# Two rows of wo per partition loaded early, in sixteen loads of eight partitions

## Chip, cores, metric

The kernel runs on one core of one Trainium2 chip. The metric is the device time of one execution in microseconds. A profile is of one further execution; its span, from the first to the last instruction, is some 2 us shorter than the device time.

## The reference

One decode step: attention over a long cache, plus a small dense block, plus the residual.

```python
q = (xn @ wq)                                   # 2 x 32 heads x 128
scores = einsum("bhqd,bhkd->bhqk", q, k_cache) * (Dh ** -0.5)
o = einsum("bhqk,bhkd->bhqd", softmax(scores), v_cache)
return x + o.reshape(B, 1, H * Dh) @ wo + relu(xn @ w1) @ w2
```

Everything is bfloat16. The caches are 2 x 32 x 8192 x 128 each: 268 MB of the 280.5 MB that the kernel reads. wo is 4096 x 512, 4 MB.

## The kernel before

The work goes in 32 pairs of (batch, head). Each pair has a K tile and a V tile of 4 MB: 128 partitions with 32 KB each. In the trace a tile is 128 packets of 32 KB (a packet is one of its DMA records) and sixteen increments of its semaphore, so eight packets for each of the 16 DMA engines. K and V have two buffers each. PE (TensorE, the matrix engine) transposes the K tile, multiplies it with q, and multiplies the V tile of the pair before with its weights. SyncE (SP) issues all large loads in one queue and waits only for buffers:

```python
        load_k(0)
        load_k(1)
        load_v(0)
        for t in range(NP - 2):
            sp.wait_ge(pT[NG - 1], t + 1)     # K tile t transposed
            load_k(t + R)
            sp.wait_ge(sW, t + 1)             # V tile t - 1 used up
            load_v(t + 1)
        ...                                   # the last V tile in two halves
        for c in range(NC):                   # wo last, in five chunks
            sl = slice(cuts[c], cuts[c + 1])
            sp.dma_start(wo_sb[:, sl, :], wo_v[:, sl, :]).then_inc(dW[c], 16)
```

wo lies in 32 rows of 512 elements (1 KB) per partition. The chunks have 14, 7, 6, 3 and 2 rows, and PE multiplies each with the attention's result as it lands, four matmuls a row:

```python
        for c in range(NC):
            pe.wait_ge(dW[c], 16)
            for j in range(cuts[c], cuts[c + 1]):
                for k in range(KT):
                    t = pe.matmul(fin[:, k, :], lhsT=wo_sb[:, j, k * P:(k + 1) * P],
                                  rhs=OX[:, j, :], start=False, stop=...)
```

## Time and profile before

| what | value | how to read it |
|---|---|---|
| time | 660.92 us (660.84 to 661.13, 6 runs) | median |
| DMA, data queue | 280.50 MB, 99.2% of 16 engines' span | busy all the time: bytes over rate set the end |
| K and V tiles | one lands every 9.71 us | 8 packets of 1.21 us, plus the semaphore write (a packet of 4 B, 9 ns) |
| K tile 4 | lands at 100.80 us | the first tile behind the place of the change |
| last wo chunk | lands at 654.85 us, last of 16 engines | first of them at 653.04 |
| end of PE's matmuls | 655.29 us | 0.44 us behind the landing |

The lines of the page and of the chain that carry this are in the prediction. What matters most is not on the page: the sixteen increments of a load's semaphore. Every load of 128 partitions has sixteen at its landing in the trace. I read each as the end of one DMA engine's share, and their spread as how far the engines have drifted apart. Before, from 130 us on, nine engines are up to 0.4 us apart, and seven are 1.7 to 1.9 us behind the first.

### The profile page before, as it was taken

The page shows a single profiled execution, that of the slowest core. Times are in us where ns is not written, and L with a number is a line of the kernel's source. Part 1 is how long each engine was busy: PE and PEld are TensorE (multiplying, and loading weights), DVE is VectorE, ACT ScalarE, POOL GpSimd, SP SyncE. Part 2 cuts the span into 40 slices and gives each one's busy share as a digit, 9 for nine tenths or more (in the row PEclk, how much of TensorE's full clock was granted, in tenths as well). Part 3 has the DMA queues.
Part 4 walks back from the last instruction along what each step waited for, and adds up shares of the span by engine and source line. Part 5 has one row for each costly group of instructions (what it writes and reads, how often), then busy time and mean ns, then how long its engine had stood idle before and what let it go on. Part 6 is the DMA issues. An engine that isn't in the chain of part 4 may idle for free.

```text
span 658.6 us, 26859 instructions
## 1 busy us (share of the span) xinstructions
PE 559.9 (85%) x12737; PEld 535.1 (81%) x12737; DVE 253.2 (38%) x436; ACT 255.8 (39%) x403; POOL 9.0 (1%) x46
## 2 busy tenths in 40 slices
PE   2998799987989878879887887997878997887896
PEld 0488798987879878879887887987878987887895
DVE  1144344442434433334443343443434443333441
ACT  1043444443433434334353434344333444333340
POOL 1000000000000000000000000000000000000000
PEclk9799999998998988999898899898989998898988
DMA  8999999999999999999999999999999999999996
GB/s 365 430 444 418 439 430 429 432 428 442 422 442 424 436 428 432 432 428 444 420 442 428 432 430 430 434 430 442 424 436 428 432 432 428 440 424 442 426 424 281
DMA packets 10542, 280.66 MB, mean 426 GB/s; under 512 B 1186, under 2 KB 1188, under 8 KB 1700
## 3 DMA queue, kind: packets, MB, share of 16 engines
q1 hardware_dynamic: 10528, 280.50, 99.2%
q8 instruction: 9, 0.15, 0.1%
q14 instruction: 1, 0.01, 0.0%
q10 hardware_dynamic: 4, 0.00, 0.0%
HBM read 280.50 MB, written 0.00 MB: 426 GB/s over the span
## 4 chain that ended last, share of the span: by engine, by line
DMA 58%; PE 37%; ACT 2%; issue 1%; SPq 1%; ACTq 0%; DVE 0%
DMA ks<-in_A_k_cache_dram 54%; PE tp L285 21%; PE Sc L292 11%; PE ot L305 4%; DMA w_sb<-in_A_wo_dram 4%; ACT kT L412 2%; ACT L412 1%; SPq L187 0%; PE Sc L340 0%; SPq L182 0%; PE Sc L343 0%; SPq L170 0%; SPq L169 0%; SPq L163 0%; PE ot L397 0%
## 5 line engine op out<-in xcount | busy, mean ns | idle before, releaser
L285 PE MATMUL tp<-identb,ks 128*128 128x128 bf16 x4096 | 323.5, 229 | 68.4 <-DMA ks<-in_A_k_cache_dram 68.4
L412 DVE COPY kT<-tp 128x1024 bf16<-128x1024 bf16 x320 | 219.7, 691 | 324.3 <-PE tp L285 324.2
L285 PEld LDWEIGHTS tp<-identb,ks 128*128 128x128 bf16 x4096 | 254.8, 102 | 72.3 <-DMA ks<-in_A_k_cache_dram 72.2
L412 ACT COPY kT<-tp 128x1024 bf16<-128x1024 bf16 x192 | 194.3, 1012 | 233.4 <-PE tp L285 233.3
L292 PE MATMUL Sc<-q,kT 128*128 128x64 bf16 x4096 | 216.8, 196 | 7.6 <-ACT kT L412 5.7
L292 PEld LDWEIGHTS Sc<-q,kT 128*128 128x128 bf16 x4096 | 178.4, 100 | 11.3 <-ACT kT L412 9.0
L305 PE MATMUL ot<-prm,vs 128*128 128x64 bf16 x4224 | 156.1, 192 | 4.2 <-issue 4.2
L305 PEld LDWEIGHTS ot<-prm,vs 128*128 128x128 bf16 x4224 | 139.0, 97 | 7.0 <-issue 4.4
L525 ACT COPY nm<-Sc 128x2 f32<-128x2 f32 x32 | 5.1, 160 | 118.5 <-PE Sc L343 118.5
L529 ACT ACTIVATE prm<-Sc,nm 64x128 bf16<-64x128 f32 x64 | 25.7, 401 | 4.3
L466 DVE TENSOR_REDUCE mcol<-Sc 64x1 bf16<-64x128 f32 x64 | 18.6, 290 | 18.7 <-PE Sc L292 18.3
L412 ACT ACT_TABLE_LOAD x16 | 20.5, 1283 | 2.2
L240 PE MATMUL ot<-vs,xz 128*16 128x512 bf16 x32 | 9.5, 470 | 8.6 <-DMA vs<-in_A_wq_dram 8.6
L517 ACT COPY OTf<-ot 128x2 f32 x32 | 5.1, 160 | 26.9 <-PE ot L305 26.9
L471 DVE TENSOR_REDUCE mx<-Sc 1x2 bf16<-1x128 bf16 x32 | 8.9, 278 | 16.9 <-PE Sc L340 16.9
L240 PEld LDWEIGHTS ot<-vs,xz 128*16 128x16 bf16 x32 | 3.3, 105 | 14.4 <-issue 12.2
L225 POOL COPY q<-qb 128x2 bf16<-128x2 bf16 x32 | 5.8, 184 | 588.9 <-PE Sc L292 566.1
L529 ACT ACTIVATION_READ_ACCUMULATOR prm<-Sc,nm x64 | 11.8, 185 | 0.0
L442 DVE TENSOR_SCALAR qs<-ot 16x512 bf16<-16x512 f32 x1 | 0.7, 679 | 18.0 <-PE ot L240 18.0
L340 PE MATMUL Sc<-identb,mcol 128*1 128x128 bf16 x32 | 7.0, 217 | 0.0
L270 PE MATMUL Sc<-w_sb,hT 128*2 128x512 bf16 x14 | 5.8, 604 | 0.1
L343 PE MATMUL Sc<-mx,onesb 1*128 1x2 bf16 x32 | 5.5, 172 | 0.0
(56 smaller groups left out, 37.5 us busy)
## 6 DMA issues: line engine op xcount, KB each, us to landing
ks<-in_A_k_cache_dram SPq DMA_DIRECT2D x32, 4096.0 KB, 26.7
vs<-in_A_v_cache_dram SPq DMA_DIRECT2D x31, 4096.0 KB, 31.3
vs<-in_A_wq_dram SPq DMA_DIRECT2D x1, 4096.0 KB, 12.1
vs<-in_A_v_cache_dram SPq DMA_DIRECT2D x2, 2048.0 KB, 19.3
w_sb<-in_B_w_dram SPq DMA_DIRECT2D x2, 1792.0 KB, 17.9
w_sb<-in_A_wo_dram SPq DMA_DIRECT2D x1, 1792.0 KB, 25.4
w_sb<-in_A_wo_dram SPq DMA_DIRECT2D x1, 896.0 KB, 27.1
w_sb<-in_A_wo_dram SPq DMA_DIRECT2D x1, 768.0 KB, 28.5
```

Source lines behind the costliest of these rows:

```text
L225: g.tensor_copy(q2[t % R][:], qb[:, 2 * t:2 * t + 2]).then_inc(sQ1, 1)
L240: i = pe.matmul(qp, lhsT=xz[:, kt, Z - g * Bsz:Z - g * Bsz + QG * Bsz], rhs=vs[1][:, (kt * QG + g) * 512:(kt * QG + g + 1) * 512], start=( ...
L270: i = pe.matmul(y, lhsT=hT[:, j, :], rhs=w2_sb[:, j, :], start=(j == 0), stop=(j == FT - 1),)
L285: t = pe.transpose(tp[e % 4][:, i, :], ks[r][:, kk * Dh:(kk + 1) * Dh], identb[:])
L292: t = pe.matmul(Sc[r][:, 2 * kk:2 * kk + 2 * REP], lhsT=kT[e % 4][:, i, :], rhs=rep(q2[r][:]), start=True, stop=True,)
L305: t = pe.matmul(ot[r][:, 0:2 * REP], lhsT=vs[r][:, kk * Dh:(kk + 1) * Dh], rhs=rep(prm[r][:, kk, :]), start=(kk == 0), stop=(kk == KB - 1),)
L340: pe.transpose(tr_of(r), mcol[r][:], identb[:]).then_inc(sT, 1)
L343: pe.matmul(bc_of(r), lhsT=onesb[:], rhs=mx[r][:], start=True, stop=True).then_inc(sB, 1)
L412: fn(kT[e % 4][:], tp[e % 4][:]).then_inc(kR[e], 1)
L466: m = v.tensor_reduce(out=mcol[i][half, :], in_=S_of(i)[half, :, u], axis=AX.X, op=ALU.max)
L471: v.tensor_reduce(out=mx[i][:], in_=tr_of(i).rearrange("o (u m) -> o u m", u=2), axis=AX.X, op=ALU.max, negate=True,).then_inc(sX, 1)
L529: x = a.activation(out=prm[i][half, :, u], in_=S_of(i)[half, :, u], func=ACTF.Exp, bias=nm[i][half, u:u + 1], scale=1.0, accum_out=RS[half ...
```

## The change

The intent is to use that drift. Two of the 32 rows of every partition (256 KB) are taken out of the last chunks and loaded in the middle of the stream by eight of the sixteen engines alone, in 16 loads of eight partitions. The trace names no engine. I number the engines by e3 (below), where a load of n partitions ran on n engines for every n from 2 to 16 and each set lay inside the next: engine n - 1 is the one that the load of n partitions adds. That this order holds is my assumption. The low engines are 0 to 7, which carry a load of eight. If they have time to spare, the other eight have 16 KB less to carry at the end. The diff (`...` marks what is left out, here and below):

```diff
...
-    cuts = (0, 14, 21, 27, 30, WJ)
+    cuts = (0, 2, 15, 22, 28, 31, WJ)
+    LOW = 0
...
+    def load_wo(sp, c):
+        step = 8 if c == LOW else P
+        for p in range(0, P, step):
+            sl = slice(p, p + step), slice(cuts[c], cuts[c + 1])
+            sp.dma_start(wo_sb[sl], wo_v[sl]).then_inc(dW[c], 16)
...
             load_v(t + 1)
+            if t == 1:
+                load_wo(sp, LOW)
...
-        for c in range(NC):
-            sl = slice(cuts[c], cuts[c + 1])
-            sp.dma_start(wo_sb[:, sl, :], wo_v[:, sl, :]).then_inc(dW[c], 16)
+        for c in range(1, NC):
+            load_wo(sp, c)
...
-            pe.wait_ge(dW[c], 16)
+            pe.wait_ge(dW[c], 16 * (P // 8) if c == LOW else 16)
```

More of the change, by code (lines that the diff above doesn't have):

```diff
@@ L129 @@
     dH = [sem(f"dH{i}") for i in range(2)]
-    dW = [sem(f"dWo{i}") for i in range(5)]
+    dW = [sem(f"dWo{i}") for i in range(6)]
     sG, sI, sQ, sQ1 = sem("sG"), sem("sI"), sem("sQ"), sem("sQ1")
```

## The prediction

0.30 and 0.32 us less at the end and 16 x 93 ns = 1.49 us more on eight engines take the last landing from 654.85 to about 654.3, and the time from 660.91 to 660.3; with 0.1 us for the rivals it is 660.4.

> **What bounds the kernel now.** I read the page first (parts 2 to 4), then the chain of waits, the DMA queue's own waits, the stretches of the last ten microseconds, and last the sixteen increments of each load's semaphore in the trace.
>
> The page, parts 2 to 4:
>
> ```profile
> DMA  8999999999999999999999999999999999999996
> ...
> q1 hardware_dynamic: 10528, 280.50, 99.2%
> q8 instruction: 9, 0.15, 0.1%
> ...
> DMA 58%; PE 37%; ACT 2%; issue 1%; SPq 1%; ACTq 0%; DVE 0%
> ```
>
> The sixteen DMA engines are busy from the first slice to the last but one. Both directions of the argument start here: 280.50 MB is fixed by the problem, the change adds and removes no byte, so only two things can move: idle time of DMA engines, and what follows the last landing. The last slice (16.5 us) is only 6 tenths busy. The end of the chain, in order of time:
>
> ```profile
> 625.73 29.12 DMA w_sb<-in_A_wo_dram
> 654.85 0.05 issue
> 654.90 0.39 PE ot L397 x8
> 655.29 0.02 issue
> 655.31 0.18 DVE yT L502
> ```
>
> The last of the five wo loads lands at 654.85; eight matmuls (two rows of four) and a fixed output tail follow. Now the DMA share in short stretches there (columns: stretch, length, five engines' busy time with counts, clock, DMA share, GB/s):
>
> ```profile
> 651.00:652.00 1.00, 1.00 (x46) 1.00 (x44) 0.00 (x0) 0.00 (x0) 0.00 (x0) 1.00 1.01 401
> 652.00:653.00 1.00, 0.49 (x18) 0.40 (x14) 0.00 (x0) 0.00 (x0) 0.00 (x0) 1.00 0.83 326
> 653.00:653.40 0.40, 0.15 (x3) 0.07 (x4) 0.00 (x0) 0.00 (x0) 0.00 (x0) 0.68 0.53 215
> 653.40:654.00 0.60, 0.60 (x24) 0.60 (x24) 0.00 (x0) 0.00 (x0) 0.00 (x0) 0.50 0.49 191
> ```
>
> From 653.0 on half of the engines have nothing left, 1.8 us before the other half end. The sixteen increments of the last wo semaphore say the same, in us after its first:
>
> ```
> 0.00 0.02 0.13 0.15 0.16 0.18 0.35 0.40 | 1.63 1.65 1.67 1.70 1.74 1.78 1.80 1.81
> ```
>
> Eight engines end by 653.44, eight at 654.67 to 654.85. For the first weights the spread was 0.38 us in all. The late group grows one by one: the spread jumps to 1.72 us with one late engine in the K tile that lands at 32.73, and there are seven late engines from 130 us to 649 us. What comes in between are packets of the instruction queue. The DMA view of 29 to 110 us, then of 110 to 650 us:
>
> ```profile
> q1 hardware_dynamic: 1205, 34.83, 100.1%
> q8 instruction: 7, 0.11, 0.6%
> ...
> q1 hardware_dynamic: 8342, 232.78, 100.2%
> ```
>
> Seven instruction packets of 16 KB (1.02 to 1.10 us each; the first, at 29.57, also stretched the next data packet from 1.21 to 1.68 us) made seven engines late by about 1.5 us each, and since the queue never runs dry they stay late. The eighth packet, at 650.36, made the eighth. K and V tiles land every 9.71 us throughout, each at the pace of its latest engine.
>
> [...]
>
> **The change part by part.**
>
> *Removed from the end:* one wo row (1 KB) per partition from the first late chunk (14 to 13 rows) and one from the last (2 to 1). Every engine carries 8 partitions. A packet in the trace takes 535 ns at 14336 B, 272 at 7168, 234 at 6144, 121 at 3072, 84 at 2048 (medians), some 38 ns per KB; the 1 KB packets of x took 44. First chunk: 8 x 38 = 0.30 us less. Last chunk: 8 x (84 - 44) = 0.32 us less. All engines that got no early rows end about 0.6 us sooner (16 KB of 4096 KB/16 = 256 KB less).
>
> *Added at 72 us:* on each of 8 engines 16 packets of 2 KB at 84 ns and 16 semaphore writes at 9 ns: 16 x 93 = 1.49 us. They wait in the queue behind V tile 2, which lands at 91.09, and ahead of K tile 4. That the sum is so near the 1.5 us of one instruction packet is why I think that the change was fitted to this skew.
>
> *Sum, if the eight low engines are the early eight:* they end at 653.04..653.44 + 1.49 - 0.6 = 653.9..654.3; the high ones at 654.67..654.85 - 0.6 = 654.1..654.25. Both groups meet, and the last landing goes from 654.85 to about 654.3. Mean work per engine is the same; 0.55 us of the 1.5 us skew's idle time is won.
>
> *After the landing:* four matmuls instead of eight. In the last chunks 24 weight loads took 0.72 us, so four are 0.12 us. Against that, PE has less slack: it was through 84 matmuls at 653.09 and would now have 88 to do before the chunk of 6 rows, landing near 653.0. 24 + 12 + 4 matmuls at 30 to 33 ns from 653.25 on give 654.5, the last 4 after the landing at 654.3 as well. So PE's last matmul moves by 0.6 to 0.7 us, and the output tail stays.
>
> *SP:* the issues that are there take 0.33 to 0.44 us each (the output store of 8 partitions 0.37) with 0.05 between. Sixteen take 16 x 0.42 = 6.7 us, from 71.96 to 78.7. K tile 4 was issued at 83.61, after PE's transposes, so SP is back 4.9 us early.
>
> *Between 91 us and 643 us:* the low engines' half of K tile 4 comes 1.49 us later, level with the late half. The tile landed at 100.80 by its late engines, so it lands within 0.1 us of that. Nothing else in 500 us moves: the late engines set every landing before and after.
>
> The sum is -0.6 us of 660.91, or 660.3; I add 0.1 for the cases below.
>
> **The rivals.**
>
> *The low engines are not the early ones.* Then one late engine gets 1.49 us more and 0.6 us less: 654.85 + 0.9, so 661.8. One low engine among the late is enough. For the good case: the eight instruction packets went to eight different engines, which a blind draw from sixteen would do about one time in eight (16·15·...·9 / 16^8 = 0.12), so they seem to walk a fixed set of eight[...]; and the author's sizes fit it. Against: nothing in the trace names an engine.
>
> *One more instruction packet.*[...] On a late engine it costs 1.5 - 0.6 = +0.9 us; and the packet of 650.36 may fall on an engine without slack. Each is a small chance.
>
> *SP becomes the bound.* If the small loads took 1.1 us each,[...] K tile 4 would be issued after 90 us, V tile 2 would be the last in the queue, and all sixteen engines would idle until it comes. The DMA queue's own waits speak against it: SP waits 429.8 us for PE's transposes in 30 waits. It would cost 1 to 3 us.
>
> *The end is PE's.* If PE falls behind the late chunks, the gain shrinks to 0.3 us.
>
> **Range and chances.** I give 0.72 to the meeting of the two groups (660.0 to 660.7), 0.2 to a late engine made later, by either of the first two rivals (661.6 to 661.9), the rest to no effect or to SP. The three runs of before lie within 0.3 us. Two per cent is 13 us; no mechanism here is above 3 us, so the same within 2% has 0.98.
>
> **What would show it right or wrong.** Right: at the last wo semaphore the sixteen increments lie within 0.6 us instead of 1.81; the share of DMA stays above 0.8 until some 0.4 us before the last landing; that landing at about 654.3; K tile 4 still issued near 83.6; nine instruction packets. From the K tile of 100.8 on, spread below 0.6 us. Wrong: a spread of 3 us at the end with early engines still 1.5 us ahead (low engines were late ones), a tenth instruction packet, SP's issue of K tile 4 after 86 us, or a gap between the last landing and the last matmul over 0.6 us.

## The result, and the profile after

The changed kernel took 663.80 us (662.87 to 664.15, 6 runs) beside 660.92 us: 2.9 us slower, which is 0.4%. Ratios in this document are the mean time of one kernel's fast runs over that of the other's in the same rounds, so not quite the ratio of the medians quoted; here it is 1.0040, with a 95% interval of 1.0027 to 1.0053. "The same within 2%" was right. The predicted 660.4 us and the range up to 661.9 us were wrong.

Where the time goes is plain from the landings. The tiles up to K tile 3 land as before (K tile 3 at 81.58 us, before at 81.38). V tile 2, which was issued ahead of the early rows and carries none of them, lands at 92.37 us instead of 91.09, already 1.3 us late. K tile 4 lands at 104.23 us instead of 100.80, 3.4 us late. From there to the last V half nothing more is lost or won: a tile every 9.71 us again, 3.4 us late. The last wo chunk lands at 657.62 instead of 654.85, 2.8 us late, so the 0.6 us that were to be won at the end did come. The whole loss arises in a few microseconds around 90 us.

There the rate drops. Short stretches of the kernel before, then of the changed kernel (columns: stretch, length, busy time with counts of PE, its weight loads, VectorE, ScalarE and GpSimd, PE's granted clock, DMA share, GB/s):

```profile
88.00:90.00 2.00, 2.00 (x47) 1.86 (x43) 0.37 (x1) 1.10 (x4) 0.00 (x0) 1.00 0.88 377
90.00:92.00 2.00, 1.79 (x43) 1.76 (x43) 1.07 (x3) 1.04 (x2) 0.00 (x0) 1.00 1.18 508
92.00:94.00 2.00, 2.00 (x51) 2.00 (x48) 1.30 (x3) 1.18 (x2) 0.00 (x0) 1.00 0.91 393
```

```profile
88.00:90.00 2.00, 1.79 (x36) 1.62 (x34) 1.20 (x2) 1.17 (x2) 0.00 (x0) 1.00 1.02 316
90.00:92.00 2.00, 2.00 (x51) 2.00 (x49) 0.78 (x2) 1.30 (x2) 0.00 (x0) 1.00 1.06 275
92.00:94.00 2.00, 2.00 (x50) 2.00 (x48) 1.38 (x2) 0.93 (x2) 0.00 (x0) 1.00 0.81 279
```

Single stretches waver, since a packet of 32 KB is counted at one instant (in slices of 0.2 us the rate jumps between 0, 164 and other multiples of 164 GB/s, one such packet); but the three together moved 2.56 MB before and 1.74 MB after (2 us times the sum of the last column), a third less, while the engines counted as busy all along. So they were not waiting for work: their packets took longer. In the trace, the 32 KB packets that started from 88.9 to 96 us took 1.213 to 1.224 us before; after, 42 of 70 took over 1.3 us, and the time above 1.213 us adds up to 21.0 us of engine time. The 2 KB packets took 84 to 255 ns, 113 at the median, where I had reckoned with 84. Large packets of engines that were carrying no small ones were stretched too, as V tile 2 shows.

The second thing to see is who carries the small packets. Six engines begin with them between 88.8 and 89.1 us, when the early engines are through with V tile 2; two begin at 91.05 us. Two of the eight low engines were late ones. The increments of K tile 4, in us after the first (landing of the last in brackets):

```
before (100.80)  0.00 0.11 0.11 0.20 0.20 0.20 0.23 0.24 0.35 0.36 1.69 1.72 1.73 1.76 1.79 1.81
after  (104.23)  0.00 0.08 0.15 0.17 1.25 1.44 1.50 1.60 1.61 1.62 1.69 1.75 1.81 1.86 3.64 3.65
```

Two engines stand 1.8 us behind all others, and they stay last to the end (3.50 and 3.52 us at the last wo chunk, the next at 2.19), and each tile lands with them.

Third, SP. Its timeline in the kernel before (one line), then in the changed kernel:

```profile
83.61 0.33 SPq L158 DMA_DIRECT2D ks<-in_A_k_cache_dram  x1
```

```profile
70.81 0.33 SPq L162 DMA_DIRECT2D vs<-in_A_v_cache_dram  x1
71.18 5.44 SPq L169 DMA_DIRECT2D w_sb<-in_A_wo_dram  x16
82.79 0.36 SPq L159 DMA_DIRECT2D ks<-in_A_k_cache_dram  x1
```

Sixteen issues in 5.4 us, and K tile 4 is issued at 82.79, earlier than the 83.61 of before. SP cost nothing.

The end of the chain of waits, whose counterpart is shown in the prediction:

```profile
647.90 5.49 PE ot L314 x128
...
654.89 3.52 PE ot L406 x128
658.41 0.02 issue
658.43 0.18 DVE yT L511
```

Before, the chain ended with the last wo load and eight matmuls. Here PE comes to wo only at 654.89, when most of it has landed, runs all 128 matmuls in a row, and ends 0.79 us behind the last landing instead of 0.44. The 128 matmuls on the last V tile took 5.5 us, where the kernel before needed 4.1:

```profile
644.58 4.08 PE L305 MATMUL ot<-prm,vs 128*128 128x64 bf16 x128
```

The stretch in the changed kernel shows a cause:

```profile
648.00:652.00 4.00, 4.00 (x95) 4.00 (x93) 0.00 (x0) 0.00 (x0) 0.00 (x0) 0.63 0.97 403
```

PE was granted 0.63 of its clock there; in the kernel before that drop came at 653 us (0.68 from 653.0, 0.50 from 653.4). Where it falls differs from one execution to the next (e4, below, has 1.00 in the same stretch and ends 0.31 us behind its last landing), so these 0.35 us belong to this profile rather than to the change.

The count of instruction packets stayed at nine, so the tenth that I had feared didn't come.

### The profile page after: what moved, and what is told of

Its sections match the earlier page's. It is cut to its first block, busy times and chain, and to the rows that moved or that the text cites. A ratio compares the mean times of both kernels' runs of the same rounds, so it can differ in the third digit from the quotient of the medians.

```text
span 661.8 us, 26875 instructions
## 1 busy us (share of the span) xinstructions
PE 560.3 (85%) x12737; PEld 538.6 (81%) x12737; DVE 253.2 (38%) x436; ACT 255.8 (39%) x403; POOL 9.0 (1%) x46
## 4 chain that ended last, share of the span: by engine, by line
DMA 62%; PE 35%; ACT 2%; issue 1%; SPq 0%; DVE 0%; ACTq 0%
DMA ks<-in_A_k_cache_dram 62%; PE tp L294 21%; PE Sc L301 10%; PE ot L314 3%; ACT kT L421 1%; PE ot L406 1%; ACT L421 0%; PE ot L372 0%; PE Sc L369 0%; PE Sc L349 0%; SPq L178 0%; SPq L177 0%; PE Sc L352 0%; SPq L171 0%; PE Sc L392 0%
## 5 line engine op out<-in xcount | busy, mean ns | idle before, releaser
L314 PEld LDWEIGHTS ot<-prm,vs 128*128 128x128 bf16 x4224 | 140.5, 98 | 7.0 <-issue 4.4
L352 PEld LDWEIGHTS Sc<-mx,onesb 1*128 1x128 bf16 x32 | 2.9, 90 | 1.7
```

The source lines that it names most:

```text
L314: t = pe.matmul(ot[r][:, 0:2 * REP], lhsT=vs[r][:, kk * Dh:(kk + 1) * Dh], rhs=rep(prm[r][:, kk, :]), start=(kk == 0), stop=(kk == KB - 1),)
L352: pe.matmul(bc_of(r), lhsT=onesb[:], rhs=mx[r][:], start=True, stop=True).then_inc(sB, 1)
```

## The experiments

Theories, all mine: **A**, crowding: by where they write, the engines of a small load get in each other's way and in that of other engines. **B**: small packets are slow by themselves. And the **placement** theory, beside either: the low engines include late ones. All kernels but e1, e2, e3, e7 and e11 leave some rows unloaded or misplaced, or load them into a scratch tile; the comparison passed them all the same (presumably two rows of 32 of a small term stay below its tolerance), so "correct" says nothing for those.

**e1, rows of a load four partitions apart.** The edit, with the right result:

```diff
-        for p in range(0, P, step):
-            sl = slice(p, p + step), slice(cuts[c], cuts[c + 1])
...
+        cols = slice(cuts[c], cuts[c + 1])
...
+        for first in range(0, P, 32):
+            for p in range(first, first + 4):
+                sl = slice(p, p + 29, 4), cols
...
```

> The changed kernel, but the eight rows of each of the 16 small loads lie four partitions apart instead of side by side; same bytes, packets and engines, right result. Theory A[...]: the 2 KB packets fall from a median of 113 ns to under 95 ns, the stretched 32 KB packets near 90 us become few, K tile 4 lands at 101.8 to 102.9 us (before 100.80, changed 104.23), and the time is 661.4 to 662.6 us, since two low engines are still late ones. Theory B (small packets of 2 KB at a 32 KB pitch in HBM slow everybody): nothing changes, K tile 4 at 104 us, time 663.5 to 664.

Measured: 662.99 us (662.57 to 663.22) beside 660.85, ratio 1.0031; K tile 4 at 104.02 us. Neither theory had it. The 2 KB median did fall to 84 ns, but 41 large packets were still stretched, by 18.1 us in all. The trace says when: all 71 small packets that started before 89.92 us took 84 to 86 ns, and there the slow ones began. The first engine was due at its ninth load, the first to partition 64 and up, at about 89.42 us (an estimate: eight packets of some 86 ns from 88.73 us on). In e4 and e8, below, the slow packets also begin some half a microsecond after the small loads do (0.51 and 0.44 us). So it seems to matter which partitions an engine writes to, not only how they lie in one load; e5 and e8 test it.

**e2, the early rows in one load on all engines** (`step = P`, right result).

> The changed kernel, but the two early rows go in one load of 128 partitions on all sixteen engines. Theory A and the placement theory (low engines that were already late got more): no crowd and no extra work for any engine, so 8 x 84 ns are added to all at 91 us and taken off at the end: K tile 4 lands at 101.5 us, last landing at 654.8 to 655.0, time 660.6 to 661.1. Theory B (small packets at a wide pitch are slow in themselves): 2 KB packets over 110 ns, time over 661.5.

Measured: 660.71 us (660.66 to 660.91) beside 660.85, ratio 0.9999; K tile 4 at 101.60, last chunk at 654.95, all 2 KB packets at 84 to 88 ns. Theory B in its plain form is out: the same bytes from the same places in packets of the same size cost nothing in one load that covers all partitions.

**e3, engines numbered by marker loads.** Into the kernel before went two sets of these, into a scratch tile:

```python
        for n in range(2, 17):
            w = 256 + 8 * n
            sp.dma_start(mk[0:n, at:at + w], K_all[0:n, 0:w]).then_inc(dM, 16)
            at += w
```

> The kernel before plus two sets of 15 marker loads into a scratch tile, of 2 to 16 partitions with a packet size for each, before the first K tile and after V tile 7; nothing reads them.[...] Placement theory: among engines 0 to 7 two are late at V tile 7 and among 8 to 15 five. The premise of my prediction (the low eight are early): none of 0 to 7 is late. Time 662 to 664 us, it is not the point.

Measured: 665.80 us (one run; 662 to 664 was expected, which wasn't the point). The second set could be read almost without a gap: 133 of its 135 marker packets begin within 4 ns after another packet ended, a load of n partitions ran on n engines for every n from 2 to 16, and each set lay inside the next. That gives the engines their numbers. But the markers of the first set drew the engines 3 us apart, so early and late must be traced back through the steps of 1.5 us by which single engines fall behind. The steps that can be followed, by my tracing over gaps of a few ns, fall on engines 13, 14, 5, 9, one of 6 and 8 (10 ns apart), and one of 1 and 10 (20 ns apart). None falls on 0, 2, 3, 4 or 7. That fits two late ones among the low eight but doesn't prove it by itself; the next runs do.

**e4, source spread, destination side by side** (source rows `q:q + 29:4`, destination `p:p + 8`; wrong).

> The changed kernel, but the source rows of each small load lie four partitions' rows apart in HBM while the destination stays eight neighbouring partitions; the result is wrong on purpose. Theory A[...]: as slow as the changed kernel, 2 KB packets over 105 ns, K tile 4 at 103.5 to 105 us, time 663 to 664.3. Theory B (pitch in HBM): like the kernel with spread rows, 661.5 to 662.6 us.

Measured: 663.42 us (663.31 to 663.69), ratio 1.0038; K tile 4 at 104.43, 2 KB median 113.5 ns, 38 stretched packets, 19.6 us above normal. As the changed kernel: the spacing of the source rows plays no part. Set beside e1 it shows more. The first eight loads of both bring the same source rows, and only the destination differs: in the first 0.69 us (eight packets of 86 ns) e4's small packets took up to 104 ns, e1's 84 to 86.

**e5, partitions 0 to 63 alone, rows four apart.** The loads bring the rows of these partitions twice, the second time into a scratch tile:

```diff
...
+        for to in (wo_sb, again):
+            for first in (0, 32):
+                for p in range(first, first + 4):
+                    rows = slice(p, p + 29, 4)
+                    sp.dma_start(to[rows, cols], wo_v[rows, cols]).then_inc(dW[c], 16)
```

In the expectation, theory A's forecast comes first.

> The changed kernel, but the 16 small loads bring only the rows of partitions 0 to 63, twice (the second time into a scratch tile), with the eight rows of a load four partitions apart[...]. Packets, bytes and engines are those of the changed kernel; the result is wrong on purpose.[...] all 2 KB packets at 84 to 90 ns, the engines that carry no small loads are undisturbed, and only the two low engines that were late already (5 and 6 by the numbered run) get 1.5 us more: K tile 4 lands at 102.1 to 102.5 us, time 661.6 to 662.3 us. Small-load theory (sixteen small loads are slow by themselves, wherever they go): K tile 4 at 103.5 us or later, time over 662.8.

Measured: 662.47 us (662.13 to 662.91) beside 660.86, ratio 1.0022; K tile 4 at 103.16. **e8, the mirror**: the same with `first in (64, 96)`, so partitions 64 to 127. Here too theory A's forecast comes first; "the same" at the end means the same as e5.

> [...]the 16 small loads of the eight low engines bring the rows of partitions 64 to 127 twice[...]; wrong on purpose.[...] 2 KB packets at 130 to 200 ns, the early engines among 8 to 15 are delayed by 1.2 to 2.4 us although they carry none of the small loads, K tile 4 at 104.5 us or later, time 664 to 666 us. If only the number of small loads counted: the same[...].

Measured: 664.17 us (663.90 to 664.50), ratio 1.0048; K tile 4 at 105.11. The stretches around 90 us, e5 first, then e8:

```profile
88.00:90.00 2.00, 2.00 (x58) 1.81 (x55) 0.28 (x1) 0.58 (x3) 0.00 (x0) 1.00 0.79 323
90.00:92.00 2.00, 2.00 (x56) 2.00 (x53) 0.00 (x0) 1.09 (x5) 0.00 (x0) 1.00 1.26 431
92.00:94.00 2.00, 1.79 (x40) 1.62 (x38) 1.29 (x2) 1.04 (x2) 0.00 (x0) 1.00 0.85 360
```

```profile
88.00:90.00 2.00, 1.79 (x37) 1.62 (x35) 1.29 (x2) 1.01 (x1) 0.00 (x0) 1.00 1.10 289
90.00:92.00 2.00, 2.00 (x51) 2.00 (x49) 0.69 (x1) 1.51 (x2) 0.00 (x0) 1.00 1.20 278
92.00:94.00 2.00, 2.00 (x50) 2.00 (x48) 1.38 (x2) 0.93 (x2) 0.00 (x0) 1.00 1.07 286
```

Same engines, packet sizes, bytes and number of loads. What differs is the destination, and with it the source, the other half of wo's rows; but e2 read those rows in packets of 84 to 88 ns, and e4 beside e1 shows what the destination does alone. In e8 the rate stays under 290 GB/s for 6 us, the 2 KB packets take 158 ns at the median, and 39 large packets are stretched by 32.9 us in all. Among these are nine that started at 88.96 to 89.55 us and took 2.1 to 2.3 us, while the six early low engines were busy with small packets: so they are other engines'. In e5 the 2 KB median is 84 ns, and only 12 large packets are stretched (7.2 us); the others are undisturbed but for a few packets of 1.29 to 1.32 us. V tile 2, issued ahead of the small loads, tells the same: it landed at 91.26 us in e5 and at 93.33 in e8 (91.09 before). So the destination decides, as theory A has it; by what mechanism, no run shows. But e5 took 0.2 us more than even its upper expectation, and its K tile 4 was 0.7 us later. The rest sits in one place: after its last small packets (98 to 207 ns), each of the eight engines needs 1.88 to 2.22 us for the first 32 KB packet.

**e6, engines 0 to 3 alone** (as e5 with `slice(p, p + 13, 4)`: partitions 0 to 15 and 32 to 47).

> [...]each load has four rows, four partitions apart, so that engines 0 to 3 alone carry them, 16 packets of 2 KB each[...]; wrong on purpose, most early rows never come. By the numbered run these four are all early ones. Placement theory (the extra 1.5 us is free on an early engine and paid in full on a late one): K tile 4 lands at 100.7 to 101.0 us as in the kernel before, the last wo chunk at 654.2 to 654.5, time 660.1 to 660.5 us: what I had predicted for the change. If small loads delay others whatever they do: time over 661.

Measured: 660.57 us (660.45 to 660.72), ratio 0.9993, just above its range; K tile 4 at 101.38 and the last chunk at 654.72, both later than expected. All four engines began early (88.82 to 89.00 us), and four large packets were stretched: their first ones, 1.88 to 1.95 us. So each of them lost some 2.2 us and fell behind the late ones, by up to 0.4 us.

**e7, shorter last chunk only** (kernel before, `cuts = (0, 15, 22, 28, 31, WJ)`).

> The kernel before with its five wo chunks cut at 15, 22, 28 and 31 rows instead of 14, 21, 27 and 30, nothing early: the last chunk has one row, as in the kernel with the early rows on all engines, which was 0.14 us faster than before. If that gain is the shorter work of PE after the last landing: 660.65 to 660.8 us. If it is the early rows: 660.85.

Measured: 660.90 us (660.59 to 661.01) beside 660.86, ratio 0.9997. No gain can be told from the noise, and so none for e2 either. It also shows how far single profiles agree: with nothing early, its K tile 4 landed at 101.17 us and its last chunk at 655.13, 0.37 and 0.28 us later than in the kernel before.

**e9 and e10, what makes the first large packet long.** e9 puts one load with pieces of 2 KB in place of the 16 of e6; e10 keeps eight of them. The edit of e9 against e6, shortened:

```diff
-        for to in (wo_sb, again): ...             # 16 loads
+        sp.dma_start(again[0:13:4, :, 0:2 * D],
+            wo_v[0:13:4, 0:28].rearrange("p (a b) n -> p a (b n)", b=2)).then_inc(dW[c], 16)
```

> As the run with four engines, but in place of its 16 loads one load of four partitions, four apart, with 14 pieces of 2 KB each into a scratch tile: 14 packets on each of engines 0 to 3 and one semaphore write instead of 16; wrong on purpose. In the run with four engines the first large packet after the small ones took 1.88 to 1.95 us instead of 1.21. If that comes from the number of loads: it now takes under 1.3 us, and K tile 4 lands at 100.8 to 101.0 us by engines that carry nothing extra. If it comes from a row of small packets: it stays at 1.7 us or more.

> As the run with four engines, but with its first eight loads only: eight packets of 2 KB on each of engines 0 to 3; wrong on purpose. If the long first large packet grows with the number of small loads: 1.4 to 1.6 us. If it is a fixed cost of going from small loads to a large one: again 1.85 to 1.95 us. If it needs more than some number: 1.22.

Measured: e9 took 660.30 us (one run); its first large packets took 1.24 us. e10 took 661.56 us (one run), and its carriers' first large packets took 1.21 us (one 1.31). So the long packet goes with many separate loads and their semaphore writes (sixteen in e6); one load with 14 packets hasn't got it. What it waits for, no run shows. That eight loads are too few for it is not shown, as e10 was disturbed. PE was behind in that execution, V tile 2 was issued at 75.89 us instead of 71.63, and K tile 4 at 87.87, 1 us before the first engines were through with V tile 2. The early engines that carry nothing extra needed 1.75 to 2.06 us for their first packet of that tile. It can't be compared with the others.

**e11, the sixteen loads much later** (`if t == 20`, right result).

> The changed kernel with the 16 small loads after V tile 21 instead of V tile 2, some 370 us later, long after the seven instruction packets; the result is right. If the cost lies in the loads themselves and in the two late ones among the low engines: time 663.2 to 664.2 us as in the changed kernel, tiles landing some 3.4 us later from there on, as before until then. If it lay in the early part, where PE is the chain: under 661.5 us.

Measured: 663.43 us (663.15 to 663.43), ratio 1.0036. Near 460 us instead of 89 the cost is nearly the same, so it isn't tied to that stage or to the time of the instruction packets.

**e12 and e13, one load on four and on eight engines**, both timed; e13 is e9 with `0:29:4`.

> The one load on engines 0 to 3 again, now timed. If extra packets on early engines[...] are free, as predicted for the change: 0.4 to 0.7 us faster than the kernel before of the same rounds. If its single time of 660.30 us was luck: within 0.2 us of it.

> The same one load, but with eight partitions, four apart, so that engines 0 to 7 carry 14 packets of 2 KB each[...]; wrong on purpose. Only the late ones among the low engines can cost now: 14 x 86 ns = 1.2 us on two of them, less the 0.1 to 0.3 us by which they are ahead of the latest, less 0.6 us at the end. Placement theory: K tile 4 lands 0.9 to 1.2 us later than in its twin with four engines, last wo chunk 655.3 to 655.8 us, time 0.9 to 1.2 us over that of the twin. If all low engines were early: the same as the twin.

Measured: e12 660.22 us (660.14 to 660.49) beside 660.89, ratio 0.9989 with an interval of 0.9975 to 1.0002 (one of the nine runs of the kernel before was at 662.16 and widens it; the others lie between 660.66 and 661.19). e13 661.32 us (661.07 to 661.70), ratio 1.0004. e13's K tile 4 and time lie 1.11 and 1.10 us over those of e12, as the placement theory said; its last chunk at 655.21 is just under its range. Large packets are stretched in neither. The increments of K tile 4:

```
e12 (100.81)  0.00 0.03 0.15 0.15 0.41 0.46 1.09 1.23 1.33 1.46 1.53 1.57 1.66 1.67 1.68 1.73
e13 (101.92)  0.00 0.03 0.10 0.22 1.06 1.07 1.10 1.27 1.41 1.45 1.50 1.55 1.86 1.88 2.79 2.80
```

In e12 four of the early ten move up to the six late ones, and the tile's landing does not change. In e13 there are two engines at 2.8: the two late ones among the low eight, laid bare. By the last landing e12 gains only 0.36 us (654.49 beside 654.85), which single profiles can't tell from nothing. Its time is the better witness: the interval just includes no gain, but all five runs lie below all nine of the kernel before.

## Why the prediction was wrong

The mechanism that I built on is there. In one load to partitions 0, 4, 8 and 12, on four engines that are early, 14 packets of 2 KB each cost nothing: the median of e12 is 0.67 us below that of the kernel before, where I had said 0.5 to 0.6. But e12 leaves out most of the rows. The change itself pays three times, and the runs, each set against the kernel before of its own rounds, take it apart:

| run | engines | loads | destination (partitions) | time - before | last wo chunk lands |
|---|---|---|---|---|---|
| e12 | 0 to 3 | 1 | 0 to 12, four apart | -0.67 | 654.49 |
| e13 | 0 to 7 | 1 | 0 to 28, four apart | +0.43 | 655.21 |
| e5 | 0 to 7 | 16 | 0 to 63, four apart | +1.61 | 656.46 |
| changed | 0 to 7 | 16 | 0 to 127, neighbours | +2.88 | 657.62 |

The times of neighbouring rows do not overlap, but for one run of e5 and one of the changed kernel. The landings are of one profile each, and e7 shows that 0.3 to 0.4 us between two of them mean nothing.

- **"If the eight low engines are the early eight"** was the condition of my sum, and it failed. Two of them were late. It costs 0.7 us by the landing (e12 to e13) and 1.1 us by the time; in e13's profile PE also ended later behind the last landing (0.9 us against 0.3). I gave this rival a chance of 0.2 together with the extra instruction packet, and sized it as +0.9 us, 661.8. So this step alone leaves the time within my range.
- **"16 x 93 = 1.49 us"** was the term that broke the range: I took the packet's time from a load that covers all partitions. In the changed kernel sixteen packets took 1.7 to 2.0 us on one engine, the large packets behind them were 0.9 to 1.2 us too long, and packets of engines that carried none were stretched too. The excess has two parts. Sixteen separate loads in place of one: +1.25 us by the landing (e13 to e5; some 0.2 us of it are two packets more). Other partitions, 0 to 127 in neighbours instead of 0 to 63 four apart: +1.16 us (e5 to the changed kernel; e8, with 64 to 127 alone, stands at +3.31 in time).
- The reason for the second part was not shown: the traces name neither the engine nor the partition of a packet. What they show is the effect. The same eight engines' 2 KB packets took 84 ns at the median in e5 and 158 ns in e8, and 12 large packets were stretched by 7.2 us there, 39 by 32.9 us here. In the prediction I asked only which engines carry the rows; I didn't ask which partitions they write to.
- **"Removed from the end"**, 0.6 us, was right: K tile 4 came 3.43 us late, the last chunk 2.77. **"It lands within 0.1 us of that"**, said of K tile 4, fell with the two terms above.
- **SP**: right, with room to spare (5.4 us of issues; 6.7 reckoned). **One more instruction packet**: did not come. **The end is PE's**: it took 0.35 us in the profiled run, with the clock at 0.63.
- **The chances**: I took "eight packets on eight different engines" as a sign of a fixed set that is the low half. The observation holds (eight increments of the last wo chunk were 1.63 to 1.81 us late), the inference does not: two of the eight early-row engines began at 91.05 us, with the late ones.

What could be won at all was not shown. In e12 early packets cost nothing, but they were 56 of 2 KB where the change has 128, and they went to a scratch tile; whether all the rows can come early for nothing was not run. No right kernel here beats the kernel before beyond the noise (e2 at 660.71 beside 660.85 comes nearest).

## What to carry to other kernels

Time to spare on a DMA engine is not yet a gain: where its extra packets go counts too. Here the same eight engines with the same 16 loads cost 1.61 us with partitions 0 to 63, four apart (e5), and 3.31 us with 64 to 127 (e8), so try the destinations as well as the engines. Before one engine is given more than another, measure which engines are late; the spread of a semaphore's increments shows that some are, and marker loads with a packet size of their own can show which, if they don't disturb (in e3 the first set drew the engines 3 us apart). Take the cost of a small load from a small load of the same shape, not from a small packet in a large load (here 113 ns at the median for 84).
